# Residual load in the last attention group one output tile later; second group's feed-forward norm as a stream of its own beside the output products

## The chip, the core and the metric

The kernel runs on one core of a Trainium2 chip. A core has TensorE (products), VectorE, ScalarE, GpSimd and SyncE, which here only issues the transfers. The metric is the device time of one execution in microseconds; 683.73 us is the median of three runs before the change.

## What is computed

One transformer block with a condition: x has 2048 rows of 448 values, 16 heads of 28 values, attention over a sliding window of 256 rows, and a feed-forward part of width 1792 with Mish.

```python
def reference(A_x, A_wqkv, A_wo, B_x, B_w1, B_b1, B_w2, c, w_mod):
    ...
    x = A_x
    mod = (_silu(c) @ w_mod).reshape(c.shape[0], 6, 1, -1)
    sa, ca, ga, sb, cb, gb = (mod[:, 0], mod[:, 1], mod[:, 2], mod[:, 3], mod[:, 4], mod[:, 5])
    h = _layernorm(x, axis=-1) * (1 + ca) + sa
    x = x + ga * _A_ref(h, A_wqkv, A_wo)
    h = _layernorm(x, axis=-1) * (1 + cb) + sb
    x = x + gb * _B_ref(h, B_w1, B_b1, B_w2)
    return x
```

`_A_ref` is softmax attention in the window, then the product with `wo`; `_B_ref` is mish(h @ w1 + b1) @ w2.

## The kernel before

The 2048 rows are four groups (`NG`) of 512, each group four output tiles of 128 rows. float32 products are made of three products of parts: a value is split into a high part (`hh`, `ah`, `w2h`) and the rest (`hl`, `al`, `w2l`), so that a 128 x 512 tile of the first feed-forward product, `z`, is 11 products and a block of the second, `acc`, is 12.

**Attention.** For each head SyncE loads a query and a key tile from DRAM (`L`, `q<-scr`, `k<-scr`); TensorE makes scores `sA`, from which VectorE takes row maxima (`mx`, L691), and scores `sB`, which ScalarE exponentiates; `pv` are the products with the values. Beside the attention of a group a generator (`fill_main`) interleaves other work on TensorE; in the last group, 3, that is the output product of group 2: `gen_oT` transposes the attention's output (`ot`) and splits it (`hho`, `hlo`), `gen_wo` multiplies it with `wo`, tile by tile. Behind each tile VectorE adds the residual (`xr`, L639) and takes the statistics of the next norm (L214, L215), and SyncE stores the sum (`x1d<-xr`). The residual tiles share three buffers (tag `xr`): the load of the fourth waits for the store of the first. What is put on the list `later` is issued at fixed places of the loop, one entry at a time. Beside this `gen_w1` loads and splits the `w1` pieces.

**Feed-forward.** The loop over `n` goes through 4 groups x 14 tiles of the hidden width. In step n TensorE makes `z` of tile n (`f1_mm`; tiles 0 to 8 of group 0 are made before), ScalarE does Mish and the high part `ah`, VectorE the rest `al` (`f1_act`), `pieces` splits a further weight piece (`w2h` on ScalarE, `w2l` on GpSimd), and `ff2` makes the 12 products of tile n - 1. Between them `fill_step` advances one generator, `fill`: in group 0 that is a chain of the last attention group's `gen_oT` and `gen_wo` and then of the norm for group 1, `gen_x1_ln2(1)`; in groups 1 and 2 it is the norm of the next group. The norm (`gen_ln2`, `ln2_blocks`) scales the rows (`xn`, L244) and transposes them on VectorE in blocks, sixteen instructions (L913) for each of four column parts; then `hi` has ScalarE write `hhf` and VectorE scale `yt`, and `lo` has GpSimd write `hlf`. The buffers of `hhf` and `hlf` in group 1 are those of `hho` and `hlo`. Each engine works through its own instructions in the order in which the program issues them.

Of the kernel before, what the change touches and what calls it, by code (L numbers as in the profile page):

```python
# [15 lines left out]
NG, GT = 4, 512  # L16
# [35 lines left out]
def adaln_block(ctx: ExitStack, tc: tile.TileContext, x, wqkv, wo, w1, b1, w2, c, w_mod, out):  # L52
# [582 lines left out]
    def gen_wo(g, tag, bufs):  # L635
# [8 lines left out]
        def store(xr, t):  # L644
            j = 4 * g + t
            dma(x1d[j * 128:(j + 1) * 128, :], xr)
            if t == 0:
                later.append(lambda: xr_load(g, 3))

        for t in range(4):  # L650
# [150 lines left out]
    def lazy(f):  # L801
        yield from f()

    FW, XN2 = {}, {}
    w2h, w2l, w2p, h2, x1 = {}, {}, {}, {}, {}

    def stage(name):
# [40 lines left out]
    def gen_w1():  # L848
# [22 lines left out]
        for n in range(12):  # L871
            next(ln, None)
            yield
            w1_hi(n)
            w1_lo(n, POOL)
            if n % 4 == 3:
                w1_cols[0] += D
            next(ln, None)
            yield
            if n == 2:  # L880
                XN2[0] = [x1[0][:, t] for t in range(4)]
            if n + 3 < 12:
                later.append(lambda n=n: w1_load(n + 3))
# [7 lines left out]
            piece_load(i)  # L891
            yield

    def ln2_blocks(g, xs, hh, hl):
        y = mid.tile([128, 4, GT], F32, name=f"yt{g}", tag="on", bufs=2)

        def hi(ci):
            ACT.activation(hh[:, ci], y[:, ci], AF.Identity, scale=cols[:, 3, ci:ci + 1], bias=cols[:, 2, ci:ci + 1])
            DVE.tensor_scalar(y[:, ci], y[:, ci], cols[:, 3, ci:ci + 1], cols[:, 2, ci:ci + 1],
                               op0=ALU.mult, op1=ALU.add)  # L900

        def lo(ci):
            POOL.tensor_tensor(hl[:, ci], y[:, ci], hh[:, ci].bitcast(F32), op=ALU.subtract)

        for ci in range(4):
            yield from blocks(XN2[g], y, ci, lambda ci=ci: hi(ci), lambda ci=ci: lo(ci))

    def blocks(x, y, ci, *stages):
        x4 = x.rearrange("p t (c n) -> p t c n", c=4)
        y4 = y.rearrange("p c (t n) -> p c t n", t=4)  # L910
        for n in range(16):
            i, j = divmod(n, 4)
            DVE.transpose(y4[32 * j:32 * j + 32, ci, :, 32 * i:32 * i + 32],  # L913
                          x4[32 * i:32 * i + 32, :, ci, 32 * j:32 * j + 32])
            if j == 3:
                if i == 3:
                    pipe.add(1, *stages)
                yield

    def gen_ln2(g, pl, xn_tiles, tag, bufs):  # L920
        xs = None
        for r in gen_ln([x1[g][:, t, 0:D] for t in range(4)], pl, xn_tiles, f"f{g}", mv=mv2[g]):
            xs = r or xs
            yield 0.6
        hh, hl = h2[g] = new_T(f"f{g}", (mid, FW.get("ff"))[g % 2])
        if g == 1:
            yield
        yield from ln2_blocks(g, xs, hh, hl)

    def gen_ln2_0():  # L930
        while 0 not in XN2:
# [308 lines left out]
    for i in range(4, 9):  # L1240
        piece_load(i)
    chunk["v"] = 6
    fill = chain(gen_oT(NG - 1, "tr", 2, ff), gen_wo(NG - 1, "tr", 2), finish(), gen_x1_ln2(1))

    def fill_step():
        if fill is not None:
            pipe.step()
            next(fill, None)
            flush()
    for n in range(NN + 1):  # L1250
        g, f = divmod(n, NF)
        if f == 0 and n:
            while fill is not None and next(fill, "END") != "END":
                pipe.step()
            fill = None
            while pipe.items:
                pipe.step()
        if n == ZN:
            x1_load(0, p1)
        if f == 2 and 0 < g < NG - 1:  # L1260
            fill = gen_x1_ln2(g + 1)
        if 2 <= n < NN:
            if n not in zs:
                f1_mm(n, "z")
# [5 lines left out]
        if n:  # L1270
            fill_step()
            ff2(n - 1)
            for _ in range(2 + (g == 0)):
                fill_step()
    for st in (ff_s, mid_s, cst_s, FW["s"], psf_s):
        st.close()

# [22 lines left out]
```

## Time and profile before

| | |
|---|---|
| median of 3 runs | 683.73 us (681.36 to 686.13) |
| the profiled execution | 681.16 us, its span 679.4 us |
| TensorE busy | 640.9 us (94%) |
| VectorE busy | 389.7 us (57%) |
| ScalarE busy | 341.1 us (50%) |
| GpSimd busy | 123.5 us (18%) |
| mean granted clock of TensorE | 0.985 |

Busy time of TensorE overlaps from product to product, so it says little on its own; what it waited for, and the granted clock (1.0 is 2.4 GHz, 0.5 is 1.2 GHz), are read beside it.

### The profile page before, as it was taken

How to read it: one execution, taken by the hardware profiler on the slowest of the kernel's cores; microseconds unless marked ns; L12 is line 12 of the kernel's file. 1: busy time of each engine (PE TensorE's matmuls, PEld its weight loads, DVE VectorE, ACT ScalarE, POOL GpSimd, SP SyncE). 2: the span in 40 equal slices, each digit the busy share in tenths (PEclk: the TensorE clock that was granted, in tenths of full speed). 3: DMA queues.
4: the chain of work that ended last, by engine and by line, in shares of the span. 5: the costliest groups of instructions: out<-in, count | busy, mean ns of one | idle time of the engine just before them, and what ended most of it. 6: DMA issues, size and time to landing. Idle time of an engine off the chain costs nothing.

```text
span 679.4 us, 10742 instructions
## 1 busy us (share of the span) xinstructions
PE 640.9 (94%) x3712; PEld 511.5 (75%) x3712; DVE 389.7 (57%) x1136; ACT 341.1 (50%) x591; POOL 123.5 (18%) x175
## 2 busy tenths in 40 slices
PE   4998999999999999998789999989999999999996
PEld 3876676677877688776656679878888888888885
DVE  6865676656677677568566135974385328641112
ACT  4454576678775677735575564432243223422221
POOL 6641010133011100000122124541012001100002
PEclk9999999699999999999979999999999999999999
DMA  8775875446854478534654346203000200010001
GB/s 224 220 229 196 261 260 161 128 136 209 269 145 141 137 225 296 143 105 135 191 150 126 90 150 218 81 1 108 1 1 0 91 20 0 1 54 1 1 0 54
DMA packets 49473, 84.23 MB, mean 124 GB/s; under 512 B 5886, under 2 KB 27916, under 8 KB 49420
## 3 DMA queue, kind: packets, MB, share of 16 engines
q1 hardware_dynamic: 49420, 83.56, 40.4%
q8 instruction: 29, 0.48, 0.3%
q14 instruction: 24, 0.20, 0.1%
HBM read 53.91 MB, written 29.36 MB: 123 GB/s over the span
## 4 chain that ended last, share of the span: by engine, by line
PE 65%; DVE 14%; issue 12%; DMA 3%; ACT 3%; SPq 1%; POOL 1%; POOLq 0%; DVEq 0%; ACTq 0%
PE z L1003 12%; PE qk L321 9%; PE sA L689 6%; PE pv L771 6%; DVE junk L691 5%; PE sB L733 5%; PE acc L1217 4%; PE acc L1216 4%; PE acc L1215 4%; PE wo L321 3%; PE qk_v L321 3%; DVE yt L913 3%; PE z L321 2%; PE sB L761 2%; DMA k<-scr 1%
## 5 line engine op out<-in xcount | busy, mean ns | idle before, releaser
L691 DVE CUSTOM_DVE_ANT_0 junk<-sA,strip 128x384 bf16<-128x384 f32 (+2 forms) x256 | 135.6, 530 | 98.3 <-PE sA L689 84.7
L736 ACT ACTIVATE P<-sB 128x512 f32<-128x512 f32 (+2 forms) x192 | 109.1, 571 | 100.2 <-PE sB L733 98.3
L1015 DVE TENSOR_TENSOR al<-t,ah 128x512 fp32r<-128x512 f32 x49 | 35.5, 725 | 123.2 <-ACT ah L1014 122.8
L689 PE MATMUL sA<-k,q 84*128 84x384 f32 (+2 forms) x256 | 94.4, 372 | 12.1 <-DVE mx L691 6.3
L1013 ACT ACTIVATE t<-z,b1c 128x512 f32<-128x512 f32 x49 | 33.7, 688 | 129.6 <-PE z L1003 118.7
L733 PE MATMUL sB<-q,k 86*128 86x384 f32 (+1 forms) x352 | 86.2, 320 | 0.0
L1217 PE MATMUL acc<-w2h,al 128*128 128x448 f32 x224 | 82.2, 367 | 2.4 <-DVE al L1015 2.4
L1216 PE MATMUL acc<-w2l,ah 128*128 128x448 f32 x224 | 82.0, 366 | 0.5 <-POOL w2l L976 0.5
L1215 PE MATMUL acc<-w2h,ah 128*128 128x448 f32 x224 | 81.9, 366 | 0.0
L1003 PE MATMUL z<-hhf,w 128*128 128x512 f32 x196 | 78.0, 398 | 0.0
L1003 PE MATMUL z<-hlf,w 128*128 128x512 f32 x196 | 77.7, 397 | 0.0
L733 PEld LDWEIGHTS sB<-q,k 86*128 86x128 f32 x352 | 60.7, 197 | 13.0 <-issue 5.0
L689 PEld LDWEIGHTS sA<-k,q 84*128 84x128 f32 x256 | 48.9, 192 | 24.0 <-DVE mx L691 15.6
L913 DVE STREAM_TRANSPOSE yt<-xn 32x128 f32<-32x128 f32 x192 | 58.1, 303 | 2.6
L1003 PE MATMUL z<-hhf,w1l 128*128 128x512 f32 x147 | 58.2, 396 | 0.0
L741 ACT ACTIVATE sB<-strip 128x512 f32<-128x512 bf16 (+2 forms) x95 | 54.6, 575 | 3.0
L771 PE MATMUL pv<-P,v 128*32 128x256 f32 (+2 forms) x704 | 51.4, 405 | 0.1
L1217 PEld LDWEIGHTS acc<-w2h,al 128*128 128x128 f32 x224 | 42.1, 188 | 6.8 <-DVE al L1015 3.5
L1216 PEld LDWEIGHTS acc<-w2l,ah 128*128 128x128 f32 x224 | 42.1, 188 | 5.8 <-POOL w2l L976 1.2
L1215 PEld LDWEIGHTS acc<-w2h,ah 128*128 128x128 f32 x224 | 42.1, 188 | 4.9
L1003 PEld LDWEIGHTS z<-hlf,w 128*128 128x128 f32 x196 | 36.8, 188 | 8.8
L1003 PEld LDWEIGHTS z<-hhf,w 128*128 128x128 f32 x196 | 36.9, 188 | 8.2 <-issue 0.8
(168 smaller groups left out, 1083.9 us busy)
## 6 DMA issues: line engine op xcount, KB each, us to landing
k<-scr SPq DMA_DIRECT2D x48, 252.0 KB
q<-scr SPq DMA_DIRECT2D x64, 168.0 KB
scr<-st SPq DMA_DIRECT2D x21, 512.0 KB
scr<-st SPq DMA_DIRECT2D x29, 256.0 KB
x<-x1d SPq DMA_DIRECT2D x10, 448.0 KB
xin<-in_A_x_dram SPq DMA_DIRECT2D x8, 448.0 KB
xr<-in_A_x_dram SPq DMA_DIRECT2D x16, 224.0 KB
x1d<-xr SPq DMA_DIRECT2D x16, 224.0 KB
```

Of the source, the lines that this page charges most:

```text
L321: PE.matmul(p, b, a, start=(n == 0), stop=(n == 10))
L689: PE.matmul(p[:, c0:384], q[0:84, t * 128:(t + 1) * 128], k[0:84, t * 128 + c0:t * 128 + 384], start=True, stop=True)
L691: DVE.tensor_tensor_reduce(out=junk[:, c0:384], in0=p[:, c0:384], in1=mask[:, c0:384], scale=1.0, scalar=-3.0e38, op0=ALU.add, op1=ALU.max ...
L733: PE.matmul(p[:, c:c + 128 * (t1 - t0)], k[:, jj * 128:(jj + 1) * 128], q[:, t0 * 128:t1 * 128], start=False, stop=True, skip_group_check= ...
L736: ACT.activation(P[:, c0:], p[:, c0:], AF.Exp, scale=SCALE)
L741: ACT.activation(p[:, c0:], strip[:, c + c0:c + 512], AF.Copy)
L771: PE.matmul(pvb[q][32 * a:32 * a + 32, t0 * 128:t1 * 128], V[j % NV][:, h + a, :], Pt[4 * w + a][:, c:c + 128 * (t1 - t0)], start=(b == 0 ...
L913: DVE.transpose(y4[32 * j:32 * j + 32, ci, :, 32 * i:32 * i + 32], x4[32 * i:32 * i + 32, :, ci, 32 * j:32 * j + 32])
L1003: PE.matmul(zb[n], ps[m][1], ps[m][0], start=(m == 0), stop=(m == 10))
L1215: PE.matmul(p, ah[n][:, ts], w2h[f], start=(f == 0), stop=False)
L1216: PE.matmul(p, ah[n][:, ts], w2l[f], start=False, stop=False)
L1217: PE.matmul(p, al[n][:, ts], w2h[f], start=False, stop=(f == NF - 1))
```

## The change

In the attention group in which group 2's output product is made (`NG - 2`), the load of the fourth residual tile is put on the list behind the store of tile 1 instead of tile 0. In the feed-forward of group 0 the chain is cut in two: `gen_out` (transposes and output product) and, from step 2 on, the norm of group 1, which `fill_step(k)` advances in turn with the first (one step of the first before `ff2`, and after it the steps 0, 1, 1, 0). The norm gives way after every four transposes as before, but the sixteenth and the hand-over to `hi` and `lo` are apart now, and `hi` is only handed over once the output product has been issued (`wo_end`), since its buffers are shared with it. `gen_w1` gives way until a piece has been put in the queue before it splits it.

```diff
--- before.py
+++ after.py
@@ -644,7 +644,7 @@
         def store(xr, t):
             j = 4 * g + t
             dma(x1d[j * 128:(j + 1) * 128, :], xr)
-            if t == 0:
+            if t == (1 if g == NG - 2 else 0):
                 later.append(lambda: xr_load(g, 3))
 
         for t in range(4):
@@ -801,7 +801,7 @@
     def lazy(f):
         yield from f()
 
-    FW, XN2 = {}, {}
+    FW, XN2, wo_end = {}, {}, [False]
     w2h, w2l, w2p, h2, x1 = {}, {}, {}, {}, {}
 
     def stage(name):
@@ -871,6 +871,8 @@
         for n in range(12):
             next(ln, None)
             yield
+            while n not in w1p:
+                yield
             w1_hi(n)
             w1_lo(n, POOL)
             if n % 4 == 3:
@@ -891,41 +893,42 @@
             piece_load(i)
             yield
 
-    def ln2_blocks(g, xs, hh, hl):
+    def ln2_blocks(g):
         y = mid.tile([128, 4, GT], F32, name=f"yt{g}", tag="on", bufs=2)
 
         def hi(ci):
+            if g not in h2:
+                h2[g] = new_T(f"f{g}", (mid, FW["ff"])[g % 2])
+            hh = h2[g][0]
             ACT.activation(hh[:, ci], y[:, ci], AF.Identity, scale=cols[:, 3, ci:ci + 1], bias=cols[:, 2, ci:ci + 1])
             DVE.tensor_scalar(y[:, ci], y[:, ci], cols[:, 3, ci:ci + 1], cols[:, 2, ci:ci + 1],
                                op0=ALU.mult, op1=ALU.add)
 
         def lo(ci):
+            hh, hl = h2[g]
             POOL.tensor_tensor(hl[:, ci], y[:, ci], hh[:, ci].bitcast(F32), op=ALU.subtract)
 
         for ci in range(4):
-            yield from blocks(XN2[g], y, ci, lambda ci=ci: hi(ci), lambda ci=ci: lo(ci))
-
-    def blocks(x, y, ci, *stages):
+            yield from blocks(XN2[g], y, ci)
+            while not wo_end[0]:
+                yield
+            pipe.add(1, lambda ci=ci: hi(ci), lambda ci=ci: lo(ci))
+            yield
+
+    def blocks(x, y, ci):
         x4 = x.rearrange("p t (c n) -> p t c n", c=4)
         y4 = y.rearrange("p c (t n) -> p c t n", t=4)
         for n in range(16):
             i, j = divmod(n, 4)
             DVE.transpose(y4[32 * j:32 * j + 32, ci, :, 32 * i:32 * i + 32],
                           x4[32 * i:32 * i + 32, :, ci, 32 * j:32 * j + 32])
-            if j == 3:
-                if i == 3:
-                    pipe.add(1, *stages)
+            if j == 3 and i < 3:
                 yield
 
     def gen_ln2(g, pl, xn_tiles, tag, bufs):
-        xs = None
         for r in gen_ln([x1[g][:, t, 0:D] for t in range(4)], pl, xn_tiles, f"f{g}", mv=mv2[g]):
-            xs = r or xs
             yield 0.6
-        hh, hl = h2[g] = new_T(f"f{g}", (mid, FW.get("ff"))[g % 2])
-        if g == 1:
-            yield
-        yield from ln2_blocks(g, xs, hh, hl)
+        yield from ln2_blocks(g)
 
     def gen_ln2_0():
         while 0 not in XN2:
@@ -1240,25 +1243,32 @@
     for i in range(4, 9):
         piece_load(i)
     chunk["v"] = 6
-    fill = chain(gen_oT(NG - 1, "tr", 2, ff), gen_wo(NG - 1, "tr", 2), finish(), gen_x1_ln2(1))
-
-    def fill_step():
-        if fill is not None:
+    def gen_out():
+        yield from gen_oT(NG - 1, "tr", 2, ff)
+        yield from gen_wo(NG - 1, "tr", 2)
+        wo_end[0] = True
+
+    fill = [gen_out()]
+
+    def fill_step(k=0):
+        if fill:
             pipe.step()
-            next(fill, None)
+            if k < len(fill):
+                next(fill[k], None)
             flush()
     for n in range(NN + 1):
         g, f = divmod(n, NF)
         if f == 0 and n:
-            while fill is not None and next(fill, "END") != "END":
-                pipe.step()
-            fill = None
+            for k in range(len(fill)):
+                while next(fill[k], "END") != "END":
+                    pipe.step()
+            fill = []
             while pipe.items:
                 pipe.step()
         if n == ZN:
             x1_load(0, p1)
-        if f == 2 and 0 < g < NG - 1:
-            fill = gen_x1_ln2(g + 1)
+        if f == 2 and g < NG - 1:
+            fill.append(gen_x1_ln2(g + 1))
         if 2 <= n < NN:
             if n not in zs:
                 f1_mm(n, "z")
@@ -1270,8 +1280,8 @@
         if n:
             fill_step()
             ff2(n - 1)
-            for _ in range(2 + (g == 0)):
-                fill_step()
+            for k in (0, 1, 1, 0) if g == 0 else (0, 0):
+                fill_step(k)
     for st in (ff_s, mid_s, cst_s, FW["s"], psf_s):
         st.close()
```

On SyncE in the last attention group, behind the load of `w1` piece 2 (`xr9` to `xr11` are group 2's residual tiles 1 to 3, `q2` and `k3` the head loads, `x1d` the stored sum), before:

```order
L59 DMA xr11_4057<-in_A_x_dram 128x448
L59 DMA q2_1_391<-scr_81 84x512
L59 DMA k3_2_376<-scr_81 84x768
L59 DMA x1d_82<-xr9_3866 128x448
L59 DMA q2_1_391<-scr_81 84x512
L59 DMA k3_3_377<-scr_81 84x768
L59 DMA w1p3_4139<-in_B_w1_dram 64x448 x2
```

And now:

```order
L59 DMA q2_1_391<-scr_81 84x512
L59 DMA k3_2_376<-scr_81 84x768
L59 DMA x1d_82<-xr9_3866 128x448
L59 DMA q2_1_391<-scr_81 84x512
L59 DMA k3_3_377<-scr_81 84x768
L59 DMA xr11_4130<-in_A_x_dram 128x448
L59 DMA w1p3_4139<-in_B_w1_dram 64x448 x2
```

The residual load `xr11` has gone from ahead of two heads' loads to behind them.

On VectorE at the start of the feed-forward stage (`al5` to `al8` are the rests of hidden tiles 5 to 8, `wo3_2` and `wo3_3` the output tiles 2 and 3 of the last group, `yt1` the transposed norm of group 1), before:

```order
L1015 TENSOR_TENSOR al5_5061<-zx_4635,ah5_5060 128x512
L639 TENSOR_TENSOR xr15_4995<-xr15_4995,wo3_3_5047 128x448
L214 BN_STATS stw33_5072<-xr15_4995 128x6
L215 BN_AGGR mv2_3_404<-stw33_5072 128x2
L244 TENSOR_SCALAR xn2_1_5091<-x1_1_4837,mv2_1_402,rsf1_5088 128x448
L1015 TENSOR_TENSOR al6_5094<-zx_4635,ah6_5093 128x512
L244 TENSOR_SCALAR xn2_1_5091<-x1_1_4837,mv2_1_402,rsf1_5088 128x448 x3
L1015 TENSOR_TENSOR al7_5126<-zx_4635,ah7_5125 128x512
L913 STREAM_TRANSPOSE yt1_5136<-xn2_1_5091 32x4x32 x16
L1015 TENSOR_TENSOR al8_5166<-zx_4635,ah8_5165 128x512
L899 TENSOR_SCALAR yt1_5136<-yt1_5136,cols_182 128x512
```

And now:

```order
L639 TENSOR_TENSOR xr14_4985<-xr14_4985,wo3_2_5052 128x448
L214 BN_STATS stw32_5078<-xr14_4985 128x6
L215 BN_AGGR mv2_3_404<-stw32_5078 128x2
L923 STREAM_TRANSPOSE yt1_5082<-xn2_1_4969 32x4x32 x8
L1018 TENSOR_TENSOR al6_5100<-zx_4635,ah6_5099 128x512
L639 TENSOR_TENSOR xr15_5028<-xr15_5028,wo3_3_5092 128x448
L214 BN_STATS stw33_5128<-xr15_5028 128x6
L215 BN_AGGR mv2_3_404<-stw33_5128 128x2
L923 STREAM_TRANSPOSE yt1_5082<-xn2_1_4969 32x4x32 x8
L904 TENSOR_SCALAR yt1_5082<-yt1_5082,cols_182 128x512
L1018 TENSOR_TENSOR al7_5145<-zx_4635,ah7_5144 128x512
L923 STREAM_TRANSPOSE yt1_5082<-xn2_1_4969 32x4x32 x8
```

The first sixteen transposes have moved from behind `al7` to ahead of it, in eights, between the additions of output tiles 2 and 3.

On ScalarE behind hidden tile 6 (`hhf1` is the high part of group 1's norm, the instructions from `zx` to `zx` are Mish of tiles 7 and 8), before:

```order
L1014 ACTIVATE ah6_5093<-zx_4635 128x512
L975 ACTIVATE w2h6_5098<-w2p6_4909 128x448
L1010 ACTIVATE zx_4635<-zx_4635 128x512
L1014 ACTIVATE ah7_5125<-zx_4635 128x512
L975 ACTIVATE w2h7_5130<-w2p7_4948 128x448
L1010 ACTIVATE zx_4635<-zx_4635 128x512
L1014 ACTIVATE ah8_5165<-zx_4635 128x512
L975 ACTIVATE w2h8_5170<-w2p8_4952 128x448
L898 ACTIVATE hhf1_5123<-yt1_5136,cols_182 128x512
```

And now:

```order
L1017 ACTIVATE ah6_5099<-zx_4635 128x512
L978 ACTIVATE w2h6_5104<-w2p6_4908 128x448
L903 ACTIVATE hhf1_5140<-yt1_5082,cols_182 128x512
L1013 ACTIVATE zx_4635<-zx_4635 128x512
L1017 ACTIVATE ah7_5144<-zx_4635 128x512
L978 ACTIVATE w2h7_5149<-w2p7_4944 128x448
L1013 ACTIVATE zx_4635<-zx_4635 128x512
L1017 ACTIVATE ah8_5176<-zx_4635 128x512
```

`hhf1` of the first column part now stands ahead of Mish of tile 7.

## Rows read from the trace of the kernel before

**Rows 1.** Waits of TensorE, whole span: line, releaser, us in total, times, longest.

```profile
PE sA L689 <- DMA k<-scr: 4.3, 2, 3.6
...
PE acc L1217 <- DVE al L1015: 2.4, 3, 1.1
...
PE acc L1216 <- POOL w2l L976: 0.5, 2, 0.3
```

**Rows 2.** SyncE's issues around the key load: start us, us, engine, line, transfer, count.

```profile
328.63 1.00 SPq L59 DMA_DIRECT2D w1p<-in_B_w_dram  x2
334.75 0.33 SPq L59 DMA_DIRECT2D xr<-in_A_x_dram  x1
...
335.59 0.38 SPq L59 DMA_DIRECT2D k<-scr  x1
```

**Rows 3.** Waits of SyncE from 318 to 350 us.

```profile
SPq L59 <- DMA x1d<-xr: 5.0, 1, 5.0
```

**Rows 4.** Busy time by stretches, then granted TensorE clock, DMA share, GB/s.

```profile
100.00:120.00 20.00, 18.47 (x115) 12.81 (x113) 13.02 (x51) 12.82 (x26) 0.71 (x3) 0.99 0.58 172
120.00:130.00 10.00, 9.63 (x52) 6.13 (x52) 4.97 (x17) 5.63 (x9) 0.94 (x1) 0.50 0.25 77
328.00:334.00 6.00, 5.28 (x31) 4.32 (x30) 4.24 (x15) 1.98 (x4) 0.00 (x0) 1.00 0.91 286
336.00:340.00 4.00, 0.76 (x5) 0.53 (x3) 1.24 (x6) 3.46 (x7) 1.93 (x5) 1.00 0.82 236
341.00:349.00 8.00, 7.26 (x41) 4.88 (x40) 4.67 (x17) 4.17 (x8) 1.61 (x3) 0.57 0.65 191
```

**Rows 5.** DMA issues of the whole span: transfer, count, KB of each.

```profile
k<-scr SPq DMA_DIRECT2D x48, 252.0 KB
q<-scr SPq DMA_DIRECT2D x64, 168.0 KB
```

**Rows 6.** TensorE's timeline, last attention group; [idle before <- releaser].

```profile
340.33 0.41 PE L689 MATMUL sA<-k,q 84*128 84x384 f32 x1 [3.57 <-DMA k<-scr]
...
344.05 0.69 PE L689 MATMUL sA<-k,q 84*128 84x384 f32 x1 [0.74 <-DVE mx L691]
344.67 1.94 PE L771 MATMUL pv<-P,v 128*32 128x256 f32 x16
...
386.77 1.07 PE L771 MATMUL pv<-P,v 128*32 128x256 f32 x16
```

**Rows 7.** VectorE's timeline, addition of output tile 3 (residual tile 11).

```profile
342.05 0.62 DVE L639 TENSOR_TENSOR xr<-xr,wo 128x448 f32<-128x448 f32 x1
```

**Rows 8.** TensorE's timeline at the start of the feed-forward stage.

```profile
404.77 0.47 PE L1216 MATMUL acc<-w2l,ah 128*128 128x448 f32 x1 [0.20 <-POOL w2l L976]
...
418.09 0.36 PE L321 MATMUL wo<-wo,hho 128*128 128x448 f32 x1
...
421.33 0.36 PE L1215 MATMUL acc<-w2h,ah 128*128 128x448 f32 x1
```

**Rows 9.** VectorE's timeline at the start of the feed-forward stage.

```profile
420.44 0.62 DVE L639 TENSOR_TENSOR xr<-xr,wo 128x448 f32<-128x448 f32 x1 [3.25 <-DMA xr<-in_A_x_dram]
...
421.86 0.66 DVE L1015 TENSOR_TENSOR al<-zx,ah 128x512 fp32r<-128x512 f32 x1
...
427.81 5.04 DVE L913 STREAM_TRANSPOSE yt<-xn 32x128 f32<-32x128 f32 x16
432.88 0.69 DVE L1015 TENSOR_TENSOR al<-zx,ah 128x512 fp32r<-128x512 f32 x1
```

**Rows 10.** ScalarE's timeline at the start of the feed-forward stage.

```profile
408.24 0.62 ACT L1010 ACTIVATE zs<-zs 128x512 f32<-128x512 f32 x1
...
409.43 0.56 ACT L975 ACTIVATE w2h<-w2p 128x448 fp32r<-128x448 f32 x1
...
432.89 0.82 ACT L898 ACTIVATE hhf<-yt,cols 128x512 fp32r<-128x512 f32 x1 [3.12 <-DVE yt L913]
```

**Rows 11.** GpSimd's timeline at the start of the feed-forward stage.

```profile
403.57 1.14 POOL L976 TENSOR_TENSOR w2l<-w2p,w2h 128x448 fp32r<-128x448 f32 x1
```

## The prediction

> **What bounds the kernel now.** I read the waits of TensorE first, then its timeline around each wait, then the queue or engine that was late. Over the whole span it waits in a few places only, and two of them lie where the change works. The first lies in the last attention group: one wait of 3.57 us for a key load [rows 1, 6]. The second is the start of the feed-forward stage: three waits of 2.4 us together for `al` on VectorE and two of 0.5 us together for `w2l` on GpSimd [rows 1]. Between and behind them the products stand back to back to the end.
>
> The key load is late because of the queue ahead of it. SyncE issued the last of three `w1` pieces by 329.63 us and the next transfer, residual tile 11, only at 334.75 us: it takes the buffer of tile 8, whose store had to land first, a wait of 5.0 us [rows 2, 3]. The query and key load of the next head (168 and 252 KB, rows 5) stand behind it; the key load was issued at 335.59 us and TensorE could go on at 340.33 us [rows 2, 5, 6].
>
> The wait has a second price. The granted clock was full up to the wait and 0.57 on the mean over 341 to 349 us [rows 4], that is 6.9 us at the lower level (1.2 instead of 2.4 GHz): (1 - 0.57) / 0.5 x 8. The sixteen `pv` products took 1.94 us there and 1.07 us at the full clock [rows 6].
>
> **Residual load one tile later.** The store of tile 8 is no longer waited for ahead of the head loads; they can be issued at about 329.7 and 330.1 us instead of 335.2 and 335.6 us. But the queue is not empty then: between 328 and 334 us the core moved 286 GB/s, in 336 to 340 us 236 GB/s [rows 4]. What had been issued by 329.63 us was through when the store landed, at about 334.7 us. So the 420 KB follow at 236 to 286 GB/s: 1.5 to 1.8 us, to 336.2 to 336.5 us. Before, 644 KB (residual, query, key) took 2.7 us at 236 GB/s out of the 5.6 us from 334.75 to 340.33 us, so up to 2.0 us must be left for the start and the landing beyond that. The key load is usable between 336.2 and 338.5 us; I take 337.6. TensorE wants it at 340.33 - 3.57 = 336.76 us, so some 0.9 us of the wait stays (0 to 1.7).
>
> The Trainium skill speaks against the change here. DMA: Bandwidth & Descriptors, section Queues, rings and completion order, says that each DMA engine takes the descriptors of one queue in ring order. By the issue times alone the load would come 5.5 us earlier and no wait would stay; by ring order it comes 2.7 us earlier and 0.9 us stays. The 5.6 us in the rows above bear the second out.
>
> What is late next is the residual itself. It is now issued after the second key load, and behind another store, query and key load (224 + 168 + 252 KB) its own 224 KB end 3.0 to 3.7 us after the first key load: 339.2 to 342 us, I take 340.3. VectorE wants it for the addition that stood at 342.05 us [rows 7], without the wait at 338.5 us. Behind that addition stand the row maxima on VectorE that free the score banks; TensorE waits for them already, at 344.05 us [rows 6]. So the chain comes 342.05 - 340.3 = 1.75 us earlier and not 3.57 (bounds 0 and 3.6). From 344.05 us to the end of the slow stretch, at about 348.3 us, the products set the pace; at full clock half of 4.25 us goes, 2.1 us. If the clock still falls, nothing of that comes. **Attention: 3.9 us gained, bounds 0 and 5.7.**
>
> **Norm of group 1 as its own stream.** No instruction is added to or taken from the group's arithmetic: the same 64 transposes, in eights instead of sixteens, begin earlier. Sixteen took 427.81 to 432.88 us, 5.07 us [rows 9], and `al` stood behind them. With eight (2.53 us) it comes in time in later tiles, so the three waits on `al` go. Each wait also costs the overlap with the product before it: a product starts every 0.2025 us (16 in 418.09 to 421.33 us, rows 8) though it is busy 0.36, and the first after a wait is busy 0.47. So each is 0.27 us dearer than its idle time. Removed: 2.4 + 3 x 0.27 for `al`, and 0.3 + 0.27 for the longer `w2l` wait [rows 1] = 3.8 us. In eights the transposes cost nothing beyond that: with `al` and the scaling VectorE has some 3.6 us of work in a tile for which TensorE needs 23 products, about 5 us; were that cover gone, the 1.1 us waits would be back.
>
> The rest moves without a price. On SyncE the residual load of tile 14 goes ahead of the store of tile 12; it waits for `al` 4 at about 414 us instead and is wanted at about 422 us, so 5 us cover it. The copies on GpSimd are the same four, spread out. The guard in the weight stream moves no row on any engine.
>
> A new wait arises. In the new order VectorE does: addition and statistics of output tile 2, eight transposes, `al` 6, addition and statistics of tile 3, eight transposes; only then has ScalarE its input for `hhf`, and behind `hhf` stand Mish 7, `ah` 7 and `w2h` 7, and behind those `w2l` 7 on GpSimd. Before, Mish 7 and 8 came ahead of `hhf`. From the end of output tile 2 this chain takes:
>
> - addition and statistics 1.42 us (420.44 to 421.86), twice: 2.84 [rows 9]
> - sixteen transposes: 5.07 [rows 9]
> - `al`: 0.66 [rows 9]
> - `hhf`: 0.82; Mish to the start of `w2h`: 1.19; `w2h`: 0.56 [rows 10]
> - `w2l`: 1.14 [rows 11]
> - seven handovers of some 0.05 us: 0.35
>
> Together 12.6 us. TensorE has in that time eleven products of output tile 3, two blocks of 12 products (tiles 5 and 6) and one more: 36 x 0.2025 = 7.3 us. So it waits 5.3 us at `acc` of tile 7. Another 0.4 us is lost at the start: the second block waits for `w2l` 1 until 404.77 us in any case [rows 8, 11], and two transposes stood in front of it where one stands now. At the last tile `hlf` waits behind two `w2l` on GpSimd, some 0.2 us. New: 5.9 us, against 3.8 removed: **2.1 us lost** (bounds 1.5 and 3).
>
> TensorE then stands still for about 5.3 us, longer than the 3.57 us after which the granted clock fell for 6.9 us. Here nothing but TensorE bounds the work behind the wait, so 6.9 us at half speed cost 3.4 us. Bounds: 0 if the clock holds, 5 if the stretch is like that of 120 to 130 us, 10 us at 0.50 [rows 4]. **Feed-forward: 5.5 us lost.**
>
> **Sum.** -3.9 + 5.5 = +1.6 us against the profiled execution (span 679.4, time 681.16 us); as the median of the runs is 683.73 us, I put the same difference on it: 685.3 us. About 1%, 6.8 us, is what a measurement of this kernel can tell from no change. I forecast no change.
>
> **The rivals.**
> - The clock holds behind the new wait. For it: waits of 1.1 us in the feed-forward left it full. Against: the one longer wait before did not. Then -3.9 + 2.1: 681.9 us.
> - Slower: the clock falls in the last attention group all the same, and behind the new wait too. For it: from 120 us on it was at 0.50 for 10 us after a stretch in which TensorE was busy 18.47 of 20 us [rows 4], so a long wait is not needed; with the residual late TensorE stands still for 2 us or more near 341 us. Against: the only fall in this group came after the long wait. It decides when the residual lands after 340.5 us. Gain 0 to 1.75 us, loss 5.5: 687.5 to 689.2 us.
> - The key load comes in time, the residual too, and the wait at tile 7 is shorter than 5.3 us because an output tile is done earlier: up to 5.7 gained and 1.5 lost, 679.5 us. As times of the runs spread from 681.36 to 686.13 us, the long key wait may also be what differs between them; then up to 8 us are gained, 676 us.
>
> TensorE: Matmul & The Clock Gate in the Trainium skill, section What's actually happening, says that the slow clock is the default state, that activity releases it and that idleness brings it back. By that alone the slower rival falls away, since its idle times are short, and the forecast stands at 685.3 us. The trace agrees in the stretch behind the key wait, not in the one from 120 us, before which TensorE was busy.
>
> **How the numbers follow.** Since rows 4 hold one fall behind a long wait and one without, the clock falls more likely than not behind 5.3 us, and is open in the attention group: forecast 0.42, clock holds 0.25, slower 0.20, better than both 0.13. The likeliest alone gives 683 to 687 us. Leaving out the outer ends of the last two, the range is 678.5 to 689.5 us. Faster by over 1% is below 676.9 us: 0.08, a part of the last case. Slower by over 1% is above 690.6 us: 0.08, if the slow stretch is 10 us long and the attention gains nothing. Within 1%: 0.84.
>
> **What would show it.** Right: no wait on the key load over 1 us near 337 us, a wait on the residual by VectorE; the three waits on `al` gone; one wait of about 5 us of TensorE on `w2h` or `ah` of tile 7 with a granted clock of 0.5 behind it. Wrong: no wait over 2 us at tile 7, or a transposition stream that begins before output tile 2 is added; or the key wait still 3 us, because what was queued takes longer than I count.

## The result and the profile after

The changed kernel takes 686.78 us (median of 20 runs, 683.58 to 689.65) against 683.73 us of the kernel before (median of 20, 680.17 to 687.55). The ratio is 1.0046 with a 95% interval of 1.0027 to 1.0064, that is 3.1 us more (1.8 to 4.4): slower, by less than the 1% that the forecast took as the bound. The profiled run took 683.58 us, its span is 681.8 us, its mean granted clock 0.983. It is the shortest of the 20: its stages are those of one execution, and the medians stand for the time.

The waits of TensorE over the whole span (line, releaser, us in total, times, longest):

```profile
PE sA L689 <- DVE mx L691: 9.1, 20, 3.4
PE acc L1218 <- ACT w2h L978: 4.2, 1, 4.2
...
PE sA L689 <- DMA k<-scr: 1.9, 2, 1.1
PE acc L1219 <- POOL w2l L979: 1.9, 2, 1.1
```

Against [rows 1] the key wait has shrunk from 3.6 to 1.1 us and the three waits on `al` are gone. In their place stand one of 3.4 us for the row maxima and one of 4.2 us for `w2h`.

A stage is best read between marks that every kernel has. I take three: `b1t`, the transposition of the bias shortly before the key load; the first product `acc`, where the feed-forward stage begins; and the end of the span. In after the marks are these rows of TensorE's timeline:

```profile
328.73 0.20 PE L869 MATMUL b1t<-ident,b1r 14*128 14x14 f32 x1 [0.32 <-DMA b1r<-in_B_b_dram]
...
399.43 0.45 PE L1218 MATMUL acc<-w2h,ah 128*128 128x448 f32 x1
```

And in before:

```profile
329.71 0.20 PE L869 MATMUL b1t<-ident,b1r 14*128 14x14 f32 x1 [0.45 <-DMA b1r<-in_B_b_dram]
...
400.31 0.45 PE L1215 MATMUL acc<-w2h,ah 128*128 128x448 f32 x1
```

So the attention part took 70.6 us before and 70.7 us after, the feed-forward stage to the end of the span 279.1 and 282.4 us. The whole loss lies in the second; the 1.0 us between the first marks lies ahead of both edits.

**Attention.** SyncE's issues of after, which answer to [rows 2]:

```profile
329.80 0.67 SPq L59 DMA_DIRECT2D k<-scr  x1
330.57 0.42 SPq L59 DMA_DIRECT2D x1d<-xr  x1
332.63 0.31 SPq L59 DMA_DIRECT2D q<-scr  x1
...
333.75 0.36 SPq L59 DMA_DIRECT2D xr<-in_A_x_dram  x1
```

SyncE's longest wait from 330 to 334 us, between the store and the query load:

```profile
SPq L59 <- DMA x<-x1d: 1.6, 1, 1.6
```

VectorE's addition of tile 3, which answers to [rows 7]:

```profile
340.92 0.62 DVE L639 TENSOR_TENSOR xr<-xr,wo 128x448 f32<-128x448 f32 x1 [2.20 <-DMA xr<-in_A_x_dram]
```

And TensorE, which answers to [rows 6]:

```profile
336.92 0.42 PE L689 MATMUL sA<-k,q 84*128 84x384 f32 x1 [1.14 <-DMA k<-scr]
...
342.93 0.69 PE L689 MATMUL sA<-k,q 84*128 84x384 f32 x1 [3.42 <-DVE mx L691]
343.54 1.94 PE L771 MATMUL pv<-P,v 128*32 128x256 f32 x16
```

The key comes in time but for 1.14 us. The residual, issued 4 us after the key load, lands only at 340.9 us; VectorE waits for it, the row maxima stand behind that addition, and TensorE waits 3.42 us for them. The wait has moved by six microseconds and kept its length. The `pv` products run at half clock as before.

**Feed-forward.** TensorE, which answers to [rows 8]:

```profile
403.87 0.47 PE L1219 MATMUL acc<-w2l,ah 128*128 128x448 f32 x1 [1.13 <-POOL w2l L979]
...
432.38 0.47 PE L1218 MATMUL acc<-w2h,ah 128*128 128x448 f32 x1 [4.16 <-ACT w2h L978]
433.64 0.74 PE L1219 MATMUL acc<-w2l,ah 128*128 128x448 f32 x1 [0.78 <-POOL w2l L979]
```

VectorE (answers to [rows 9]) and then ScalarE ([rows 10]):

```profile
421.21 0.62 DVE L639 TENSOR_TENSOR xr<-xr,wo 128x448 f32<-128x448 f32 x1 [3.14 <-PE wo L321]
...
422.63 2.48 DVE L923 STREAM_TRANSPOSE yt<-xn 32x128 f32<-32x128 f32 x8
...
425.75 0.61 DVE L639 TENSOR_TENSOR xr<-xr,wo 128x448 f32<-128x448 f32 x1
...
427.25 2.52 DVE L923 STREAM_TRANSPOSE yt<-xn 32x128 f32<-32x128 f32 x8
```

```profile
429.87 0.81 ACT L903 ACTIVATE hhf<-yt,cols 128x512 fp32r<-128x512 f32 x1 [8.73 <-DVE yt L923]
...
431.77 0.56 ACT L978 ACTIVATE w2h<-w2p 128x448 fp32r<-128x448 f32 x1
```

The first eight transposes stand between the additions of tiles 2 and 3, the second eight behind that of tile 3 (the section on the change puts all sixteen between them). ScalarE stood 8.7 us idle for `hhf`, with Mish, `ah` and `w2h` of tile 7 behind it. From the addition of tile 2 to the product that needs `w2l` of tile 7 (421.21 to 433.64 us) the chain takes 12.4 us; the sum of the prediction said 12.6.

Busy time by stretches (us, PE, PEld, DVE, ACT, POOL, then granted clock, DMA share, GB/s), which answer to [rows 4]:

```profile
340.00:348.00 8.00, 5.07 (x29) 3.40 (x30) 3.75 (x13) 3.71 (x8) 1.75 (x3) 0.57 0.45 130
432.00:438.00 6.00, 4.84 (x15) 4.05 (x16) 5.79 (x15) 1.95 (x4) 3.51 (x3) 0.72 0.21 51
```

(1 - 0.57) / 0.5 x 8 = 6.9 us at 1.2 GHz in the attention group, as before (6.8 us where a window is cut at the ends of the slow stretch, in both kernels; 0.57 is rounded). Behind the new wait it is (1 - 0.72) / 0.5 x 6 = 3.4 us.

### The profile page after: what moved, and what is told of

Its sections match the earlier page's. It is cut to its first block, busy times and chain, and to the rows that moved or that the text cites. A ratio compares the mean times of both kernels' runs of the same rounds, so it can differ in the third digit from the quotient of the medians.

```text
span 681.8 us, 10744 instructions
## 1 busy us (share of the span) xinstructions
PE 640.7 (94%) x3712; PEld 512.4 (75%) x3712; DVE 390.0 (57%) x1136; ACT 340.6 (50%) x591; POOL 122.6 (18%) x175
## 4 chain that ended last, share of the span: by engine, by line
PE 66%; issue 13%; DVE 11%; DMA 5%; POOL 2%; ACT 1%; SPq 1%; POOLq 0%; DVEq 0%; ACTq 0%
PE z L1006 13%; PE qk L321 9%; PE sA L689 6%; PE pv L771 6%; DVE junk L691 5%; PE sB L733 5%; PE acc L1219 4%; PE acc L1220 4%; PE acc L1218 4%; PE qk_v L321 3%; PE z L321 2%; PE sB L761 2%; PE wo L321 2%; DMA xr<-in_A_x_dram 2%; PE qk L506 1%
## 5 line engine op out<-in xcount | busy, mean ns | idle before, releaser
L689 PE MATMUL sA<-k,q 84*128 84x384 f32 (+2 forms) x256 | 94.2, 371 | 12.4 <-DVE mx L691 9.1
L689 PEld LDWEIGHTS sA<-k,q 84*128 84x128 f32 x256 | 48.7, 191 | 24.4 <-DVE mx L691 18.4
```

The costliest lines, as they stand in the source:

```text
L689: PE.matmul(p[:, c0:384], q[0:84, t * 128:(t + 1) * 128], k[0:84, t * 128 + c0:t * 128 + 384], start=True, stop=True)
```

## The experiments

Eleven kernels, timed beside the kernel before in four groups (e1 to e4, e5 to e7, e8 to e10, e11); between groups only the differences against before are compared. The table has the difference that follows from the ratio of the runs, with its 95% interval, and three readings of each profiled execution: the two stages by the marks above, and the time at the lower clock between `b1t` and the first `acc`. Single executions reach `b1t` between 328.7 and 333.6 us, and ahead of it the kernels differ only in when a residual tile or a `w1` piece is loaded; so the stages are compared, not the spans. A stage is that of one execution, though, and the same order of loads doesn't always take the same time: see e2.

| kernel | against before, us | attention, us | at 1.2 GHz there, us | feed-forward, us |
|---|---|---|---|---|
| before | 0 | 70.6 | 6.8 | 279.1 |
| after | +3.1 (+1.8 to +4.4) | 70.7 | 6.8 | 282.4 |
| e1 residual line alone | -0.5 (-2.2 to +1.0) | 70.4 | 6.8 | 279.1 |
| e2 norm stream alone | +3.5 (+1.8 to +5.1) | 67.6 | 3.4 | 283.7 |
| e3 `hi` one step later | -2.0 (-3.6 to -0.4) | 70.8 | 10.2 | 277.8 |
| e4 four buffers | -0.5 (-2.7 to +1.5) | 68.0 | 3.4 | 278.7 |
| e5 residual early | -3.4 (-5.0 to -1.6) | 68.8 | 6.8 | 278.4 |
| e6 stream one step earlier | -2.0 (-3.6 to -0.3) | 71.0 | 6.8 | 278.6 |
| e7 e5 and e6 | -3.1 (-4.9 to -1.2) | 67.6 | 0 | 279.3 |
| e8 e5 and a `w1` piece later | -5.9 (-7.7 to -4.0) | 66.2 | 0 | 278.5 |
| e9 e3 and e5 | -4.7 (-6.6 to -2.7) | 67.2 | 3.4 | 277.2 |
| e10 e3, e5 and e6 | -6.2 (-8.7 to -3.8) | 66.4 | 0 | 276.9 |
| e11 e10 and e8 | -6.1 (-8.3 to -3.8) | 65.4 | 0 | 276.9 |

### The two edits apart

e1 is before with one line of the change, e2 is after without that line.

```diff
--- before.py, as e1
-            if t == 0:
+            if t == (1 if g == NG - 2 else 0):
--- after.py, as e2
-            if t == (1 if g == NG - 2 else 0):
+            if t == 0:
```

> The kernel before with one line of the change: the load of the fourth residual tile goes on the list behind the store of tile 1 instead of tile 0 in the last attention group. My theory now: the wait only changes its place. TensorE's wait for the key load near 337 us shrinks from 3.57 to about 1 us, the residual lands at 341 to 342 us, VectorE's addition waits 2 us for it, TensorE then waits 3 to 3.5 us for the row maxima, and the clock falls behind that as before: 0 us against before, bounds -1 and +1 us. The prediction's term: -3.9 us (0 to -5.7).

Measured: -0.5 us (-2.2 to +1.0). VectorE's addition of tile 3 and TensorE's waits in e1:

```profile
345.37 0.62 DVE L639 TENSOR_TENSOR xr<-xr,wo 128x448 f32<-128x448 f32 x1 [1.65 <-DMA xr<-in_A_x_dram]
```

```profile
341.92 0.41 PE L689 MATMUL sA<-k,q 84*128 84x384 f32 x1 [1.29 <-DMA k<-scr]
347.37 0.69 PE L689 MATMUL sA<-k,q 84*128 84x384 f32 x1 [2.69 <-DVE mx L691]
```

The key wait is down, the wait behind the residual has taken its place, and the attention part takes 70.4 us. The gain of 3.9 us isn't there.

> The changed kernel with the residual load back behind the store of tile 0: only the norm as its own stream stays. My theory: the whole loss is in the feed-forward stage, with the wait of about 4.2 us on w2h of tile 7 and 0.8 us on w2l behind it, 3.8 us of small waits gone and some 1 to 2 us of slow clock: +2.5 to +3.5 us against before. The prediction's term: +5.5 us (1.5 to 8). Rival: the difference of the two kernels arises before, in the attention (its first wait on the key then stays at 3.57 us), and this kernel is within 1 us of before.

Measured: +3.5 us (+1.8 to +5.1). The two waits at tile 7 are those of after:

```profile
432.14 0.51 PE L1218 MATMUL acc<-w2h,ah 128*128 128x448 f32 x1 [4.16 <-ACT w2h L978]
433.40 0.74 PE L1219 MATMUL acc<-w2l,ah 128*128 128x448 f32 x1 [0.75 <-POOL w2l L979]
```

```profile
432.00:440.00 8.00, 7.11 (x19) 5.86 (x20) 6.86 (x19) 2.52 (x5) 3.50 (x3) 0.57 0.43 142
```

With equal waits the slow stretch behind them is 6.8 us here and 3.4 us in after; the stage is 1.3 us longer. So -0.5 and +3.5 us make up the +3.1 us of both edits within their intervals: the loss is the norm stream's alone.

e2 has the loads of before, but its attention part takes 67.6 us and not 70.6 us. Here a slow stretch of 3.4 us came ahead of the key load (granted clock 0.57 from 333 to 337 us); TensorE then waits 0.85 us for the key and no longer than 1.2 us in the group. So the wait of 3.57 us doesn't stand in every execution of that order, as the last rival of the prediction supposed, and an attention part alone can't tell 67.6 from 70.6 us. The order of the change was profiled four times (after, e1, e3, e6): 70.4 to 71.0 us, each with a wait of VectorE for the residual (1.3 to 2.2 us) and one of TensorE for the row maxima behind it (2.0 to 3.4 us).

### What the new wait hangs on

e3 puts one pipeline step between the transposes and `hi`, so that on ScalarE `hhf` stands behind Mish, `ah` and `w2h` of the next hidden tile. e6 leaves `hhf` where it is in after and starts the stream one step earlier, so that more of the transposes stand ahead of the additions.

```diff
--- after.py, as e3
-            pipe.add(1, lambda ci=ci: hi(ci), lambda ci=ci: lo(ci))
+            pipe.add(1, None, lambda ci=ci: hi(ci), lambda ci=ci: lo(ci))
--- after.py, as e6
-        if f == 2 and g < NG - 1:
+        if f == (2 if g else 1) and g < NG - 1:
             fill.append(gen_x1_ln2(g + 1))
```

> The changed kernel with one more step of the pipeline between the transposes and hi: the high part of a column part of the norm stands behind Mish, ah and w2h of the next hidden tile on ScalarE. My theory: the chain ahead of w2h of tile 7 no longer holds the second eight transposes and hhf, so the wait of 4.2 us there goes; what is left is a wait of about 2 us or less for al of tile 7, which stands behind the transposes on VectorE. 2 to 4 us faster than the changed kernel, -1.5 to +1 us against before. Rival: the second addition or the first eight transposes are what ScalarE is late for; then the wait stays at 3 us or more and the time that of the changed kernel.

Measured: -2.0 us against before (-3.6 to -0.4), and in the feed-forward stage 4.5 us less than after, more than the 2 to 4 us expected. TensorE's waits in it from the start of the stage on:

```profile
408.81 0.47 PE L1219 MATMUL acc<-w2l,ah 128*128 128x448 f32 x1 [1.12 <-POOL w2l L979]
435.50 0.47 PE L1220 MATMUL acc<-w2h,al 128*128 128x448 f32 x1 [1.92 <-DVE al L1018]
```

The wait on `w2h` is gone with the place of `hhf`; the second eight transposes now hold `al` instead, by 1.92 us as expected, and the clock stays full.

> The changed kernel with the norm's stream started one step earlier (from step 1 instead of 2 of group 0), all else as it is: the first sixteen transposes stand ahead of the additions of output tiles 2 and 3 on VectorE, where it waited 3 us, and hhf keeps its place ahead of Mish of tile 7 on ScalarE. My theory: the wait of 4.2 us at tile 7 comes from the transposes that stand behind the addition of tile 2 in the chain to hhf; with them done earlier hhf starts when the output product has been read, and no wait over 1.2 us is left at tile 7 (on al of tile 7): 5 to 7 us faster than the changed kernel, 2 to 4 us faster than before. Rival: the place of hhf ahead of Mish itself is what costs; then a wait of 2 us or more on w2h or ah of tile 7 stays and the time is within 2 us of the changed kernel.

Measured: -2.0 us against before (-3.6 to -0.3), by these differences 5.1 us against after. The time fell as expected and the wait on `w2h` is gone, but one of 2.31 us on `w2l` of tile 7 is there:

```profile
435.48 0.47 PE L1219 MATMUL acc<-w2l,ah 128*128 128x448 f32 x1 [2.31 <-POOL w2l L979]
```

ScalarE, VectorE and GpSimd ahead of it:

```profile
430.00 0.81 ACT L903 ACTIVATE hhf<-yt,cols 128x512 fp32r<-128x512 f32 x1 [4.20 <-DVE yt L923]
...
431.91 0.56 ACT L978 ACTIVATE w2h<-w2p 128x448 fp32r<-128x448 f32 x1
```

```profile
427.38 2.52 DVE L923 STREAM_TRANSPOSE yt<-xn 32x128 f32<-32x128 f32 x8
```

```profile
432.62 1.28 POOL L909 TENSOR_TENSOR hlf<-yt,hhf 128x512 fp32r<-128x512 f32 x1 [5.58 <-DVE yt L904]
433.86 2.69 POOL L979 TENSOR_TENSOR w2l<-w2p,w2h 128x448 fp32r<-128x448 f32 x2
```

The second eight still stand behind the addition of tile 2, and `hhf` still waits for them, 4.2 us instead of 8.7 us. But `w2h` of tile 7 is done at 432.47 us, before TensorE stops. What is late is `w2l`: on GpSimd `hlf` now stands ahead of it, and `hlf` waits for VectorE's scaling of `yt`, so `w2l` begins 1.4 us after its input is ready. In after it begins 0.1 us after it, ahead of `hlf`. At once behind `w2h`, with the 1.17 us it takes in after, it would be done at about 433.7 us, and TensorE would wait 0.5 us (an estimate from these rows; no run moves `hlf` alone). So e3 shows what holds tile 7 in after, Mish behind `hhf`; e6 shows that the transposes are part of that chain, and that with the chain shorter the queue of another engine is the limit.

### What holds the attention group

e4 gives the residual tiles a fourth buffer, with the order of before. e5 also puts the load of tile 11 on the list with the three others, two heads earlier. e8 is e5 with the second and third `w1` pieces put on the list; by SyncE's issues the second keeps its place and the third goes behind the two heads' loads.

```diff
--- before.py, as e4
-        return mid.tile([128, 512], F32, name=name, tag="xr", bufs=3)
+        return mid.tile([128, 512], F32, name=name, tag="xr", bufs=4)
--- e4, as e5
-            if ci < 3 and g < NG - 1:
+            if ci < 3 + (g == NG - 2) and g < NG - 1:
                 later.append(lambda t=ci: xr_load(g, t))
...
-            if t == 0:
+            if t == 0 and g != NG - 2:
                 later.append(lambda: xr_load(g, 3))
--- e5, as e8 (with the change's guard in gen_w1)
-        for n in range(3):
-            w1_load(n)
-            yield
+        w1_load(0)
+        yield
+        for n in (1, 2):
+            later.append(lambda n=n: w1_load(n))
+            yield
```

The fourth buffer does one thing more. The output tiles `yo` at the end of the kernel share the tag `xr`. VectorE's last additions in before, then in e4:

```profile
675.05 0.62 DVE L1221 TENSOR_TENSOR yo<-acc,gbn 128x448 f32<-128x448 f32 x1 [2.08 <-DMA out_dram<-yo]
```

```profile
669.36 2.46 DVE L1221 TENSOR_TENSOR yo<-acc,gbn 128x448 f32<-128x448 f32 x4 [0.97 <-PE acc L1217]
```

With three buffers the last one waits for a store, with four it doesn't, and the span ends 5.8 instead of 6.5 us after the last product. So 0.7 us of the feed-forward stage and of the time in e4, e5 and e7 to e11 has nothing to do with the residual loads.

> The kernel before with four residual buffers instead of three, its order unchanged: the load of the fourth residual tile waits for no store. My theory: the key load wait falls from 3.57 to 1.5 to 2 us, since 644 KB stand behind the w1 pieces instead of 420, but the residual comes in time, so no wait for it and none of 3 us for the row maxima takes its place: 1.5 to 2 us faster than before, and 3.5 to 4 us if the clock holds. Rival: the transfers themselves are the limit, not the order; then the wait on the key stays near 3 us and the time is that of before within 1 us.

Measured: -0.5 us (-2.7 to +1.5), which decides nothing: three of twelve runs took 677 to 679 us and nine 682 to 686 us, and the profiled one was of the three. In it the key wait is 2.12 us:

```profile
339.48 0.46 PE L689 MATMUL sA<-k,q 84*128 84x384 f32 x1 [2.12 <-DMA k<-scr]
```

> The kernel before with four residual buffers and the load of the fourth residual tile put on the list with the other three, so that it is issued two heads earlier, ahead of the w1 pieces; it waits for no store and stands neither ahead of the late key load nor behind it. My theory: what the change lost in the attention group is the residual that lands late behind two head loads; here the key wait falls to 1 us or less, VectorE does not wait for the residual, TensorE does not wait 2 us or more for row maxima, and from the transposition b1t to the first product of the feed-forward stage it takes 67 to 68.5 us instead of 70.6: 2 to 4 us faster than before. Rival: the w1 pieces (1.4 MB in 10 us) fill the queue whatever stands where; then a wait of 2 us or more stays on the key and the gain is under 1 us.

Measured: -3.4 us (-5.0 to -1.6). The key wait and the addition of tile 3 in it:

```profile
339.98 0.41 PE L689 MATMUL sA<-k,q 84*128 84x384 f32 x1 [1.76 <-DMA k<-scr]
```

```profile
342.05 0.62 DVE L639 TENSOR_TENSOR xr<-xr,wo 128x448 f32<-128x448 f32 x1
```

VectorE waits for no residual, and the addition stands 10.9 us behind `b1t`, against 12.3 us before and 12.2 us after. That part of the expectation holds, the attention part takes 68.8 us, just over the 68.5 us given. With the 0.7 us of the last output tile taken off, 2.7 us are gained, and the interval begins at 1.0 us: the rival's gain of under 1 us is only just excluded. The key wait is 1.8 us and not 1 us: something else than the residual is in the queue ahead of it.

> The kernel of the run e5 (residual loaded early) with one more transfer moved: of the three w1 pieces that are issued in one burst ahead of the head loads, the third (224 KB) goes behind the two heads' loads. It tells whether the 1.8 us that are left of the key wait come from the volume of that burst. My theory: at 236 to 286 GB/s 224 KB take 0.8 to 0.9 us, so the key load lands some 0.9 us earlier and its wait is 1 us or less; the time falls by 0.5 to 1.5 us against e5, about 3.5 to 5 us against before. Rival: the key load's own issue and landing set the wait; then it stays at 1.5 to 2 us and the time is that of e5 within 0.5 us.

Measured: -5.9 us (-7.7 to -4.0), 2.5 us less than e5 by these differences. There is no wait for that key any more; what is left near it:

```profile
339.04 0.41 PE L689 MATMUL sA<-k,q 84*128 84x384 f32 x1 [0.63 <-DVE ms L703]
...
341.93 0.50 PE L733 MATMUL sB<-q,k 86*128 86x384 f32 x2 [0.59 <-DMA k<-scr]
```

So the third piece ahead of the head loads was the rest of the wait, by its volume or its place in the issues (the key load is also issued some 0.5 us earlier, counted from `b1t`; no run tells the two apart). e11, with the same loads, has no such wait either. Of the other profiles with e5's loads e7 has one of 2.1 us, e10 of 1.2 us, and e9, behind a slow stretch, none. The gain is larger than the 0.9 us that 224 KB take. The clock accounts for part of it: e8's profile has no slow stretch behind `b1t`, e5's one of 6.8 us, of which up to half is lost.

### Together

e7 joins e5 and e6 (and one more step of the output product ahead of `ff2` in step 2), e9 joins e3 and e5, e10 joins e3, e5 and e6, e11 is e10 with the `w1` piece of e8. All four are built on after, with the residual load of e5 in place of the change's. No new line is in them but e7's:

```diff
             fill_step()
+            if n == 2:
+                fill_step()
             ff2(n - 1)
```

> The changed kernel with three edits: the early start of the stream as in the run before, the early residual load with four buffers, and one more step of the output product ahead of ff2 in step 2, so that TensorE has products where it waited 1.1 us for w2l. My theory: the two gains add, 4 to 7 us faster than before, with no wait over 1.5 us from the attention group to the end. Rival: the gains lie in the same disturbed executions and do not add: 2 to 3 us.

Measured: -3.1 us (-4.9 to -1.2), below the expectation and near the rival, though the interval reaches both. The wait on `w2l` of tile 7 is 2.28 us, behind `hlf` on GpSimd as in e6, and here the clock fell behind it:

```profile
430.00:434.00 4.00, 4.00 (x13) 3.42 (x12) 3.00 (x9) 0.81 (x1) 0.04 (x1) 0.58 0.59 181
```

That is 3.4 us at 1.2 GHz in a stretch that was at full clock in e6, and the stage takes 279.3 instead of 278.6 us, in spite of the 0.7 us gained at the end.

> Two edits together: the early residual load of e5 (four buffers) and the changed feed-forward order with hi one pipeline step later, as in e3. My theory: the gains add, 3.4 us (e5) and 1.3 to 2 us (e3): 4 to 6 us faster than before, with an al wait of about 1.9 us at tile 7 left. Rival: they do not add, since a slow stretch of the clock that the one removes comes back behind the other; then 2.5 to 3.5 us.

Measured: -4.7 us (-6.6 to -2.7). By the median the gains add, with the `al` wait of 1.93 us as in e3; the interval also reaches the rival's 2.5 to 3.5 us. The feed-forward stage is e3's less the 0.7 us of the last output tile.

> As e9, with the norm's stream started one step earlier besides: eight of the first sixteen transposes lie in VectorE's idle time ahead of the addition of output tile 2, and only four stand between the addition of tile 3 and al of tile 7. My theory: the wait on al of tile 7 falls from 1.9 to about 1 us: 0.5 to 1.5 us faster than e9. Rival: the scaling of yt, which waits for hhf behind w2h of tile 7, now stands ahead of al 7; the wait stays at 1.9 us or grows, and the time is that of e9 or longer.

Measured: -6.2 us (-8.7 to -3.8). The waits left at tile 7:

```profile
427.07 0.47 PE L1219 MATMUL acc<-w2l,ah 128*128 128x448 f32 x1 [0.58 <-POOL w2l L979]
427.95 0.48 PE L1220 MATMUL acc<-w2h,al 128*128 128x448 f32 x1 [0.41 <-DVE al L1018]
```

They sum to 1.0 us instead of 1.9 us, and the stage is 0.3 us shorter than in e9; the medians differ by more than that, but their intervals overlap widely.

> All of it: the feed-forward order of e10 and the attention loads of e8 (residual early, third w1 piece behind the head loads). My theory: the two stages are independent of each other, so the gains add: 2 to 3 us in the feed-forward stage (e10 against before) and 4 to 5 us in the attention group (e8): 6.5 to 9 us faster than before. Rival: the third w1 piece, which comes later, is then missed in the feed-forward order that splits w1 between other work, or the runs differ by slow stretches of the clock alone; then the time is that of e10 or e8, 6 us faster.

Measured: -6.1 us (-8.3 to -3.8). By its stages the gains add: the attention part is the shortest of all, 65.4 us, and the feed-forward stage is e10's. By the time they don't show: e8, e10 and e11 can't be told apart. In e11's profile `b1t` comes at 333.3 us, 2.9 us later than in e10, with a slow stretch ahead of it that e10 has not:

```profile
312.00:316.00 4.00, 4.00 (x29) 2.39 (x28) 3.00 (x9) 1.20 (x2) 1.63 (x3) 0.57 0.98 265
```

Its runs, 676.7 to 678.9 us, are the closest together. A difference of 1 us against e10 can't be told by 7 and 6 runs; e8, e10 and e11 are each about 0.9% faster than before, and 1.3% faster than the change.

Much of what they gain is the clock's. Over all runs the mean granted clock is 0.9879 in e8 and 0.9893 in e10, against 0.9821 in before beside them: (1 - 0.9821) / 0.5 of its span is 24.4 us at 1.2 GHz, against 16.4 and 14.5 us. If half of the difference is lost, that is 4.0 of the 5.9 us and 5.0 of the 6.2 us (an estimate, and an upper one, since TensorE stands still in a part of these stretches).

## Why the prediction was right, and where it was not

Forecast were 685.3 us and no change; measured are 686.78 us, inside the range. But the forecast stood on -3.9 + 5.5 us, and the stages show +0.1 and +3.3 us. Two terms were off in opposite directions and made up for one another, so that the number came so close is luck.

**The key wait** was rightly sized: 0.9 us predicted, 1.14 us measured, where the issue times alone gave none. The rule that the prediction took from the Trainium skill (DMA: Bandwidth & Descriptors, section Queues, rings and completion order), that the descriptors of one queue are taken in ring order, agrees here: counted from `b1t`, the key load was issued 4.8 us earlier and TensorE went on 2.4 us earlier, where ring order had 2.7 us. What is issued ahead counts, not the issue time. A sharing of the queue's rate among all that is issued would give the same; no run tells the two apart. e8 and e11 agree: with one `w1` piece less ahead the load isn't waited for. What the residual ahead of it adds is lost in the scatter: 1.1 to 1.6 us without it (after, e1, e3, e6), 1.2 to 2.1 us with it (e5, e7, e10). One figure of the working doesn't follow: 5.6 less 2.7 us leaves 2.9 us for the start and the landing, not 2.0; the load came at 337.9 us in the time of before, inside the bounds given.

**The residual** is the step that failed. It was to land at 340.3 us, with 342 us as the bound; it landed at 340.9 us, which is 341.9 us in the time of before, whose marks lie 1.0 us later. 868 KB (of 1024 bytes) followed the key load in 4.0 us, 222 GB/s, and not in the 3.0 to 3.7 us of the prediction's 286 to 236 GB/s. And SyncE was held, for which the prediction has no term: the query load ahead of the residual was issued 2.06 us after the store that stands before it, and 1.6 us of this is a wait for the landing of a row load `x<-x1d` issued near 326 us. So the addition came 0.15 us earlier and not 1.75 us, and with a wait of 3.42 us in place of 3.57 us the clock fell for 6.8 us as before. Both parts of the 3.9 us went, to the lower bound of 0. It is the mechanism of the slower rival, with its own condition, a residual after 340.5 us; its price came out, its total of 687.5 us did not, since the other term was too large.

**The removed waits** went as said: no wait on `al` is left in after.

**The new wait** is at the place named, `w2h` and `w2l` of tile 7, and has the size named: 4.16 + 0.78 us against 5.3 us. e3 shows the chain to be the cause. The wait for `w2l` at the start of the stage grew by 0.9 us, from 0.20 to 1.13 us, where 0.4 us had been counted.

**The clock behind it** is a term that no single profile sizes: 3.4 us lost at 6.9 us of half speed were forecast; the profile of after has 3.4 us at half speed, up to 1.7 us lost, and e2 with the same wait has the forecast stretch. What is left without the clock is 3.3 - 1.7 = 1.6 us in after and 4.6 - 3.4 = 1.2 us in e2, against the 2.1 us predicted (bounds 1.5 and 3): e2's lies just under them. Over all its runs e2's mean granted clock is 0.9808, against 0.9840 in before beside it: 4.6 us more at 1.2 GHz, 2.3 us if half of it is lost (0.3 to 4.2; an estimate). So of the 3.5 us that the stream alone costs (1.8 to 5.1), some 2.3 us may be the clock's, a range that holds the 3.4 us forecast as well; the whole loss of 5.5 us in the prediction lies outside the interval.

**The better case** was not had by the change, but it exists: of the 5.7 us that the prediction gave the attention group as its upper bound, e8's profile gains 4.4 us there (70.6 to 66.2), e11's 5.2 us, by loads that are moved ahead of the burst or out of it, not behind one another. With before's order at 67.6 us in e2, part of these gains is a matter of the execution.

## What to carry to other kernels

A load moved behind others on a full queue takes its wait along: ask when it will land and who wants it next, and move it ahead of the burst if a buffer can be had. Where work is drawn forward on one engine, write out what each other engine has queued behind its consumer; one pipeline step (e3) decided over 4.5 us of the stage, and where only the transposes came earlier (e6), GpSimd's order held the rest. A buffer added for one purpose serves every tile of its tag: look for what else it lets go. And read two edits by stages, but from more than one execution: here the sum hid that neither term was as large as said, and one order of loads took 67.6 and 70.6 us.

## What was not expected of the hardware

The slow stretch behind a wait has no fixed price. Behind waits of 4.16 us at the same place it lasted 3.4 us (after) and 6.8 us (e2); behind 2.3 us it lasted 3.4 us (e7) or did not come (e6). In the attention group it lasted 6.8 us around waits of 2.7 to 3.6 us (before, after, e1, e6) and behind 1.8 us (e5), 10.2 us behind 1.6 us with one of 2.0 us in it (e3), 3.4 us behind 2.1 us (e4), and did not come behind 2.1 us in e7. It stayed away in e8, e10 and e11, whose waits there are 1.2 us and less; but behind 1.2 us it lasted 3.4 us in e2 and e9.

Without a long wait it came as well: in eleven of the thirteen profiles the clock fell near 120 us, here in e10, where TensorE waited for nothing longer than 0.3 us in the 10 us before.

```profile
120.00:132.00 12.00, 11.52 (x64) 7.74 (x65) 6.34 (x24) 6.59 (x11) 1.27 (x1) 0.57 0.33 93
```

The Trainium skill (TensorE: Matmul & The Clock Gate, section What's actually happening) has idleness bring the slow clock back. The stretches behind long waits agree with that; this one, 10.2 us with TensorE busy 11.52 of 12 us, hardly does: TensorE's waits in the 10 us before come to 1.0 us together. No run here shows its cause.
